# Gated network: seven products in place of eight for the output products of four steps

## The chip, the cores and the metric

The kernel runs on one core of a Trainium2 chip. The metric is the device time of one execution in microseconds (us): the median of three runs was 850.7 (849.21 to 854.43). Five engines work side by side: TensorE (PE) multiplies matrices, VectorE (DVE), ScalarE (ACT) and GpSimd (POOL) do the elementwise work, SyncE (SP) issues the transfers.

## The reference

Three stages follow each other. A retention layer over 2 batches, 8 heads, 768 positions gives x of 1536 tokens by 512. Then comes the gated network, on which the change works, then a mixture of four experts:

```python
rms = np.sqrt(np.mean(x * x, axis=-1, keepdims=True) + 1e-06)
xn = x / rms * rms_g
g = xn @ w_gate                        # 512 x 1536
silu = g * (1.0 / (1.0 + np.exp(-g)))
val = xn @ w_val                       # 512 x 1536
x2 = silu * val @ w_out                # 1536 x 512
p = probs / (probs.sum(-1, keepdims=True) + 1e-09)
out = sum(p[:, e:e+1] * (np.maximum(x2 @ w1[e], 0) @ w2[e]) for e in range(4))
```

The weights of the gated network arrive as 64-bit floating point numbers, everything is computed in float32.

## The kernel before, in words

Each float32 operand of a matmul is split into a high part `hi`, a copy rounded to the format that PE takes, and a low part `lo`, the operand less its high part. A product is then three matmuls: hi x hi, hi x lo, lo x hi.

The gated network works on 6 units (`u`) of 256 of the 1536 inner values, and on 2 groups (`g`) of 768 tokens. One pair (u, g) is a step; there are 12, and the second group is g = 1. The tokens of a group are two blocks of 384. A step has

- gate products and value products (`winograd`): seven products instead of eight, of sums of inputs and of weights. A product is 6 matmuls of 384 columns. `use` is called when a quarter of the result is ready. For the gate DVE adds two parts into one of four buffers `s` (L583) and ACT applies the activation (L587); for the value DVE adds (L613), multiplies onto the gate's quarter (L616), ACT makes the high part `hhi` (L618) and DVE or POOL the low part `hlo` (L621);
- output products (`gated_out`): for 2 blocks x 4 tiles of outputs, 2 x 3 matmuls onto one PSUM bank (L1081 to L1083), 48 in all. DVE adds each bank to the sum over units `x2acc` in SBUF (L1090).

The next step's gate products and this step's output products are placed around each other by the main loop, in a fixed order. Weights come by transfers of pieces of 256 or 512 KB through three staging buffers `wst`, in the order of `turns`. A 64-bit piece is converted by shifting bits: ACT makes `bits` (L322), DVE does three steps (L325 on `wst`, L330 on `bits`, L337 into `top`), then gate and value weights get four sums (L353), high parts on ACT (L390) and low parts on DVE or POOL (L395). Two streams of pieces alternate; each has its own `bits` buffer, and both are PSUM banks.

The kernel writes the order of instructions on every engine itself. A planner (`Pace`) keeps a clock for each engine with a cost for each task; `fill` puts waiting tasks between the matmuls of a product, `need` brings those on which the next matmul depends to their engine. Tasks marked `PV` may go to POOL or DVE. Each engine works through its list in that order and waits at an instruction until what it needs is there.

The second network (16 units, `mixed_out` and `expert_out`) follows; `mixed_out` already computes its output products for the first group as seven products, from buffers of a pool "T". From 333 us on the order is unchanged.

## Time and profile before

| | us |
|---|---|
| median of three runs (lowest, highest) | 850.7 (849.21, 854.43) |
| the profiled execution, its own time | 849.45 |
| its span in the trace | 847.7 |
| retention and normalising | about 0 to 93 |
| gated network | about 93 to 348 |
| experts | about 348 to 848 |

The span is the time between the first and the last instruction in the trace; the run's time is 1.75 us longer than it. PE's matmuls are pipelined: each of 384 columns is shown with 0.33 us, and they start 0.17 us apart.

### The profile page before, as it was taken

The numbers are of one execution on the slowest core, as the hardware profiler recorded it, in microseconds if no ns is written. First come the engines' busy times: TensorE is split into PE (matmuls) and PEld (weight loads), VectorE is DVE, ScalarE is ACT, GpSimd is POOL, SyncE is SP. The second block draws the span as 40 slices with busy tenths as digits, with TensorE's granted clock in tenths as the row PEclk, the third lists the DMA queues.
The fourth block names the chain that finished last, engine by engine and source line by source line (L and its number), as shares of the span: only waits on it lengthen the run. The fifth ranks groups of instructions, "written<-read, shape, count | busy, mean of one in ns | idle before, by whom it ended". The sixth has DMA issues, their size and how long they took to land.

```text
span 847.7 us, 13943 instructions
## 1 busy us (share of the span) xinstructions
PE 834.1 (98%) x5167; PEld 794.8 (94%) x5167; DVE 541.1 (64%) x973; ACT 432.0 (51%) x971; POOL 584.9 (69%) x713
## 2 busy tenths in 40 slices
PE   8989999999999999899999999999999999999998
PEld 7879999999999999899999999999999999999987
DVE  4886867769686847832665565466466466556664
ACT  4788765445443546665544544544545454454421
POOL 3456847364454558969789888988988988988500
PEclk9999999999999999999999999999999999999999
DMA  8951232212122100111111011010011011101003
GB/s 272 318 161 51 76 99 75 75 56 94 51 75 75 50 26 26 39 29 32 40 38 37 27 38 38 26 51 26 26 51 32 20 50 38 38 26 38 1 13 136
DMA packets 29233, 52.37 MB, mean 62 GB/s; under 512 B 3989, under 2 KB 12725, under 8 KB 29165
## 3 DMA queue, kind: packets, MB, share of 16 engines
q1 hardware_dynamic: 28880, 51.24, 19.0%
q8 instruction: 40, 0.66, 0.3%
q10 hardware_dynamic: 284, 0.24, 0.1%
q14 instruction: 29, 0.23, 0.1%
HBM read 48.33 MB, written 3.15 MB: 61 GB/s over the span
## 4 chain that ended last, share of the span: by engine, by line
PE 88%; DVE 5%; ACT 3%; POOL 1%; issue 1%; DMA 1%; SPq 0%; DVEq 0%; ACTq 0%
PE bank L523 44%; PE bank L1231 7%; PE bank L1269 6%; PE bank L1270 6%; PE bank L1268 6%; PE cross L1231 5%; PE bank L1082 3%; PE bank L1083 3%; PE bank L1081 3%; PE bank L745 2%; POOL x2Tlo L1034 1%; PE bank L727 1%; DMA qk<-in_qk_dram 1%; DVE s L616 1%; PE bank L755 1%
## 5 line engine op out<-in xcount | busy, mean ns | idle before, releaser
L532 ACT COPY kept<-bank 128x384 f32<-128x384 f32 x168 | 80.5, 479 | 121.9 <-PE bank L523 111.2
L1208 DVE SCALAR_TENSOR_TENSOR oacc<-cross,p_sb,oacc 128x256 f32<-128x256 f32 (+1 forms) x126 | 65.6, 566 | 64.2 <-PE cross L1231 64.2
L1276 DVE SCALAR_TENSOR_TENSOR oacc<-bank,p_sb,oacc 128x512 f32<-128x512 f32 (+1 forms) x97 | 72.3, 746 | 52.1 <-PE bank L1270 52.0
L1137 POOL TENSOR_TENSOR hs<-h,hs 128x384 fp32r<-128x384 f32 x97 | 97.3, 1020 | 0.8 <-ACT hs L1135 0.8
L523 PE MATMUL bank<-x2Thi,widehi 128*128 128x384 f32 x256 | 87.7, 343 | 0.7 <-DVE kept L1114 0.7
L523 PE MATMUL bank<-x2Thi,widelo 128*128 128x384 f32 x256 | 86.1, 336 | 0.0
L523 PE MATMUL bank<-x2Tlo,widehi 128*128 128x384 f32 x256 | 86.0, 336 | 0.0
L1270 PE MATMUL bank<-plainhi,hs 128*128 128x512 f32 (+1 forms) x218 | 85.1, 390 | 0.0
L1269 PE MATMUL bank<-plainlo,hs 128*128 128x512 f32 (+1 forms) x218 | 85.0, 390 | 0.0
L1268 PE MATMUL bank<-plainhi,hs 128*128 128x512 f32 (+1 forms) x218 | 84.3, 387 | 0.0
L621 POOL TENSOR_TENSOR hlo<-s,hhi 128x384 fp32r<-128x384 f32 x48 | 52.8, 1101 | 30.8 <-ACT hhi L618 24.2
L1117 ACT ACTIVATE hs<-kept 128x384 fp32r<-128x384 f32 x54 | 28.4, 526 | 87.2 <-DVE kept L1114 87.1
L1082 PE MATMUL bank<-hlo,plainhi 128*128 128x384 f32 x192 | 64.3, 335 | 1.7 <-POOL hlo L621 1.7
L523 PE MATMUL bank<-xThi,widehi 128*128 128x384 f32 x192 | 64.4, 336 | 0.0
L523 PE MATMUL bank<-xThi,widelo 128*128 128x384 f32 x192 | 64.2, 334 | 0.0
L523 PE MATMUL bank<-xTlo,widehi 128*128 128x384 f32 x192 | 64.2, 334 | 0.0
L1081 PE MATMUL bank<-hhi,plainhi 128*128 128x384 f32 x192 | 64.1, 334 | 0.0
L1083 PE MATMUL bank<-hhi,plainlo 128*128 128x384 f32 x192 | 64.1, 334 | 0.0
L1208 DVE SCALAR_TENSOR_TENSOR oacc<-bank,p_sb,oacc 128x512 f32<-128x512 f32 x84 | 59.2, 745 | 6.4 <-PE bank L1231 6.4
L464 POOL TENSOR_TENSOR downlo<-down,downhi 128x512 fp32r<-128x512 f32 x28 | 36.3, 1296 | 37.9 <-ACT downhi L460 37.9
L395 POOL TENSOR_TENSOR widelo<-sums,widehi 128x512 fp32r<-128x512 f32 x44 | 57.7, 1310 | 5.3 <-ACT widehi L390 4.9
L1143 POOL TENSOR_TENSOR h<-h 128x384 f32<-128x384 f32 x55 | 55.9, 1017 | 4.2 <-ACT h L1156 2.2
(181 smaller groups left out, 2536.5 us busy)
## 6 DMA issues: line engine op xcount, KB each, us to landing
wst<-in_moe_w_dram SPq DMA_DIRECT2D x64, 256.0 KB, 2.7
qk<-in_qk_dram SPq DMA_DIRECT2D x12, 512.0 KB, 5.7
wst<-in_moe_w_gate_dram SPq DMA_DIRECT2D x12, 512.0 KB, 3.8
wst<-in_moe_w_val_dram SPq DMA_DIRECT2D x12, 512.0 KB, 3.9
wst<-in_moe_w_out_dram SPq DMA_DIRECT2D x12, 512.0 KB, 3.7
vk<-in_vk_dram SPq DMA_DIRECT2D x10, 512.0 KB, 5.4
out_dram<-oacc SPq DMA_DIRECT2D x11, 256.0 KB, 2.0
vk<-in_vk_dram SPq DMA_DIRECT2D x2, 256.0 KB, 4.3
```

What stands on the lines that cost most here:

```text
L523: nc.tensor.matmul(out=ps, lhsT=lhs, rhs=rhs, start=(first and j == i == 0), stop=(j == KH - 1 and i == 2), skip_group_check=not first,)
L532: nc.scalar.copy(out=t, in_=ps)
L1081: nc.tensor.matmul(out=ps, lhsT=whi[:, c], rhs=hi, start=(f == 0), stop=False)
L1082: nc.tensor.matmul(out=ps, lhsT=whi[:, c], rhs=lo, start=False, stop=False)
L1083: nc.tensor.matmul(out=ps, lhsT=wlo[:, c], rhs=hi, start=False, stop=(f == NF - 1))
L1137: 0, "PV", TB, lambda eng: eng.tensor_tensor(out=lo, in0=t, in1=hi.bitcast(F32), op=ALU.subtract), [high]
L1208: run = lambda eng: eng.scalar_tensor_tensor(out=acc, in0=ps, scalar=pe, in1=acc, op0=ALU.mult, op1=ALU.add)
L1231: nc.tensor.matmul(out=where[c], lhsT=lhs[:, cols], rhs=rhs, start=bool(i == 0 and opens and opens(c)), stop=(i == 2), skip_group_check=True,)
L1268: nc.tensor.matmul(out=ps, lhsT=hi[:, c], rhs=whi[:, cols], start=(f == 0), stop=False)
L1269: nc.tensor.matmul(out=ps, lhsT=hi[:, c], rhs=wlo[:, cols], start=False, stop=False)
L1270: nc.tensor.matmul(out=ps, lhsT=lo[:, c], rhs=whi[:, cols], start=False, stop=(f == NF - 1))
L1276: nc.vector.scalar_tensor_tensor(out=acc, in0=ps, scalar=pe, in1=acc, op0=ALU.mult, op1=ALU.add)
```

## The change

For (u, 1) with u from 1 to 4 the output products are seven products of sums of the products silu x value and of sums of the output weights. Seven products times two halves of the outputs times three matmuls make 42 matmuls.

- `seven_use` takes the place of `value_use`: it makes seven operands (high and low part each) in place of four. Four more differences (`less`) of 128x384 go to POOL or DVE, and three of them overwrite a buffer `s` in place.
- `seven_out` takes the place of `gated_out`. Each product is added twice, once per half of the outputs, so DVE adds 14 banks to `x2acc` in place of 8. One bank per half ("chain") is accumulated over o1, o6, o7, o4, another ("side") over o5 and o3, then anew over o2; each partial sum is added to `x2acc` before the next product goes onto its bank.
- `out_sums` makes four sums of output weights (128x256), two high and two low parts of 512 for each of the units.
- The products are mixed one by one with the next step's gate products: v1 v2 v5 v6 v3 v7 g1 g2 v4 o1 g5 o5 g6 o3 g3 o6 g7 o7 g4 o2 o4 (v, g, o: value, gate, output).
- The `bits` of the second stream (odd pieces from the fifth on) lie in SBUF; their PSUM bank serves the chain. The buffer `sums` is double.
- In `turns` the output weights of a unit come after the gate weights of the next one.

The order holds 4821 matmuls in place of 4845; DVE has 51 instructions more, ACT 20, POOL 25, and SP issues 139 in both. The orders are alike up to about 89 us and from about 333 us on.

DVE in the second step of unit 1, from the multiplication of the quarter of v7 (L616 before, L719 after) to the first additions to `x2acc`. Before:

```order
L616 TENSOR_TENSOR s_1589<-kept_1712,s_1589 128x384 [waits DVE_49]
L353 TENSOR_TENSOR sums_1748<-sums_1748,top_1715 128x128 [waits Pool_49]
L325 TENSOR_SCALAR wst_1649<-wst_1649 128x512 [waits DMAHW7_49,Activation_49]
L583 TENSOR_TENSOR s_1784<-bank_1777,kept_1771 128x384 [waits PE_49,Activation_49]
L330 SCALAR_TENSOR_TENSOR bits_1750<-bits_1750,wst_1649 128x512 [waits DVE_49]
L616 TENSOR_TENSOR s_1618<-bank_1680,s_1618 128x384 [waits PE_49]
L325 TENSOR_SCALAR wst_1725<-wst_1725 128x512 [waits DMAHW0_49,Activation_49]
L330 SCALAR_TENSOR_TENSOR bits_1799<-bits_1799,wst_1725 128x512 [waits DVE_49]
L583 TENSOR_TENSOR s_1829<-bank_1801,kept_1818 128x384 [waits PE_49,Activation_49,Pool_49]
L583 TENSOR_TENSOR s_1841<-bank_1764,kept_1808 128x384 [waits PE_49,Pool_49]
L337 SCALAR_TENSOR_TENSOR top_1845<-wst_1649,bits_1750 128x512 [waits Pool_49]
L1090 TENSOR_TENSOR x2acc0_1222<-bank_1849,x2acc0_1222 128x384 [waits PE_49]
```

The same place now (L639 is the addition of a gate product, L699 a low part, L785 the additions to `x2acc`, two of o1 and then two of o5; L329 is a step of the weights):

```order
L719 TENSOR_TENSOR s_1859<-kept_2001,s_1859 128x384 [waits DVE_49]
L357 TENSOR_TENSOR sums_2018<-top_2004 128x128
L341 SCALAR_TENSOR_TENSOR top_2060<-wst_1887,bits_1961 128x512
L699 TENSOR_TENSOR hlo_2029<-s_1805,hhi_2028 128x384 [waits Activation_49]
L699 TENSOR_TENSOR hlo_2042<-s_1859,hhi_2041 128x384 [waits Activation_49]
L639 TENSOR_TENSOR s_2074<-bank_2063,kept_2056 128x384 [waits PE_49,Pool_49]
L719 TENSOR_TENSOR s_1898<-bank_1972,s_1898 128x384 [waits PE_49]
L785 TENSOR_TENSOR x2acc1_1221<-chain_2091,x2acc1_1221 128x384 [waits PE_49]
L785 TENSOR_TENSOR x2acc1_1221<-bank_2092,x2acc1_1221 128x384 [waits PE_49]
L329 TENSOR_SCALAR wst_1900<-wst_1900 128x512 [waits DMAHW3_49]
L785 TENSOR_TENSOR x2acc1_1221<-bank_2119,x2acc1_1221 128x384 [waits PE_49]
L785 TENSOR_TENSOR x2acc1_1221<-bank_2123,x2acc1_1221 128x384 [waits PE_49]
```

Two low parts have come in behind the multiplication, the gate's addition L639 waits for POOL, and behind it stand the value's last multiplication (L719 s_1898) and the first additions to `x2acc`; before, three weight steps (L325, L330, L337) and two gate additions stood between the value's last multiplication (L616 s_1618) and the first L1090.

DVE near 89 us, where the first gate addition of unit 0's second step stands behind weight steps (L325, L329). Before:

```order
L616 TENSOR_TENSOR s_1106<-kept_1168,s_1106 128x384 [waits DVE_49]
L325 TENSOR_SCALAR wst_716<-wst_716 128x512 [waits DMAHW2_49,Activation_49]
L325 TENSOR_SCALAR wst_993<-wst_993 128x512 [waits DMAHW7_49,Activation_49]
L583 TENSOR_TENSOR s_1244<-bank_1237,kept_1231 128x384 [waits PE_49,Activation_49,Pool_49]
L330 SCALAR_TENSOR_TENSOR bits_1195<-bits_1195,wst_716 128x512 [waits DVE_49]
L616 TENSOR_TENSOR s_1156<-bank_1123,s_1156 128x384 [waits PE_49]
L337 SCALAR_TENSOR_TENSOR top_1259<-wst_716,bits_1195 128x512 [waits DVE_49]
```

And now:

```order
L672 TENSOR_TENSOR s_1106<-kept_1168,s_1106 128x384 [waits DVE_49]
L329 TENSOR_SCALAR wst_993<-wst_993 128x512 [waits DMAHW7_49,Activation_49]
L639 TENSOR_TENSOR s_1241<-bank_1234,kept_1229 128x384 [waits PE_49,Activation_49,Pool_49]
L334 SCALAR_TENSOR_TENSOR bits_1195<-bits_1195,wst_993 128x512 [waits DVE_49]
L672 TENSOR_TENSOR s_1156<-bank_1123,s_1156 128x384 [waits PE_49]
L329 TENSOR_SCALAR wst_716<-wst_716 128x512 [waits DMAHW2_49,Activation_49]
L334 SCALAR_TENSOR_TENSOR bits_1244<-bits_1244,wst_716 128x512 [waits DMAHW4_49,DMAHW3_49,DMAHW5_49,DMAHW1_49,DMAHW6_49,DVE_49,Pool_49]
L341 SCALAR_TENSOR_TENSOR top_1279<-wst_716,bits_1244 128x512 [waits DVE_49]
```

One of the two weight steps ahead of the gate addition (L583, now L639) has moved behind the multiplication.

The diff, cut to its core (the second network's use of a shared buffer `h7` is left out):

```diff
--- before
+++ after
@@ -213,6 +213,7 @@
     HD = DM // 2
     MORE_HS = 2
     MIXED = set(range(1, N2 - 1))
+    SEVEN = {(u, g) for u in (1,2,3,4,) for g in (1,)}
     STAGED = 3
     BIG = 3
     BANKS = 6
@@ -276,7 +277,7 @@
     turns = [wides[0], wides[1], plains[0], wides[2]]
     for u in range(1, N1):
-        turns += [wides[2 * u + 1], plains[u], wides[2 * u + 2]]
+        turns += [wides[2 * u + 1], wides[2 * u + 2], plains[u]]
     turns += [wides[2 * N1 + 1], plains[N1], plains[N1 + 1]]
     for u in range(2, N2):
         turns += [wides[2 * N1 + u], plains[N1 + u]]
@@ -318,7 +319,10 @@
             w = got["t"].rearrange("p h f -> p (h f)").bitcast(U32).rearrange("p (n two) -> p n two", two=2)
             got["low"], got["high"], got["hf"] = w[:, :, 0], w[:, :, 1], w[:, :, 1].bitcast(F32)
-            got["one"] = bits_pools[second].tile([P, NC], U32, tag="bits", name="bits")
+            if second:
+                got["one"] = pools["T"].tile([P, 2 * TB], U32, tag="h7", name="bits", bufs=1)[:, 0:NC]
+            else:
+                got["one"] = psum_bits.tile([P, NC], U32, tag="bits", name="bits")
             eng.activation(out=got["one"].bitcast(F32), in_=got["hf"], func=AF.Copy, scale=REBIAS)
         def sign(eng):
@@ -344,7 +348,7 @@
-                got["s"] = wconv.tile([P, 4, P], F32, tag="sums", name="sums", bufs=1)
+                got["s"] = wconv.tile([P, 4, P], F32, tag="sums", name="sums")
@@ -414,7 +418,7 @@
-                    before = sums_done[-1:] if i == 0 else []
+                    before = (sums_done[-2:-1] if double else sums_done[-1:]) if i == 0 else []
@@ -425,6 +429,10 @@
+        if key[0] == "o" and any((key[1], x) in SEVEN for x in range(G)):
+            outs[j] = got, [hi, *lows], tops[-1][0]
+            if j == NF - 1:
+                out_sums(key[1], then)
@@ -432,6 +440,52 @@
+    outs = {}
+
+    def out_sums(u, then):
+
+        (upper, dep0, free0), (lower, dep1, free1) = outs[0], outs[1]
+        key = "S", u
+
+        def sums(eng, i):
+            (a11, a21), (a12, a22) = ((x["t"][:, 0], x["t"][:, 1]) for x in (upper, lower))
+            o, x, y, op = (
+                (a22, a21, a22, ALU.add), (a21, a11, a21, ALU.subtract),
+                (a11, a22, a11, ALU.subtract), (a12, a12, a11, ALU.subtract),
+            )[i]
+            eng.tensor_tensor(out=o, in0=x, in1=y, op=op)
+
...
+        gate = lambda: "T" in pools and (("S", u - 1) not in ready or ("S", u - 1) in used)
+        last, lows = (), []
+        for i, deps in enumerate((dep1, dep0, (), ())):
+            last = [then("PV", HD, lambda eng, i=i: sums(eng, i), *last, *deps)]
+        free0 += last
+        free1 += last
+        before = last
+        for half in range(2):
+            hi = then("A", 512, lambda eng, half=half: high(eng, half), *before, gate=gate)
+            before = [hi]
+            lows.append(then("PV", 512, lambda eng, half=half: low(eng, half), hi))
+        free0.append(lows[0])
+        free1.append(lows[1])
+        ready[key] = lows
+
@@ -463,7 +517,9 @@
-        gate = lambda: "T" in pools and (u == min(MIXED) or u - 1 in sums_used)
+        gate = lambda: "T" in pools and (
+            all(("S", x) in used for x, g in SEVEN) if u == min(MIXED) else u - 1 in sums_used
+        )
@@ -625,6 +681,117 @@
+    def seven_use(s, hs):
+        t, done, read = {}, {}, {}
+        def tile(n):
+            pool, tag = (*((pools["hp"], nm) for _ in range(5) for nm in ("hhi", "hlo")), *(
+                (pools["T"], nm) for nm in ("hx", "hx", "h00", "h01")
+            ))[n]
+            return pool.tile([P, TB], F32R, tag=tag, name=tag, bufs=5 if tag in ("hhi", "hlo") else MORE_HS if tag == "hx" else 1)
+        def operand(n, at, dep):
+            hi, lo = tile(2 * len(hs)), tile(2 * len(hs) + 1)
+            src = t[at]
+            high = pace.add(0, "A", TB, lambda eng: eng.copy(out=hi, in_=src), [dep])
+            low = pace.add(
+                0, "PV", TB, lambda eng: eng.tensor_tensor(out=lo, in0=src, in1=hi.bitcast(F32), op=ALU.subtract), [high]
+            )
+            s[at][2].extend([high, low])
+            hs[n] = hi, lo, low
+            read[at] = [high, low]
+        def less(at, x, y, *deps):
+            out, x, y = t[at], t[x], t[y]
+            done[at] = pace.add(
+                0, "PV", TB, lambda eng: eng.tensor_tensor(out=out, in0=x, in1=y, op=ALU.subtract), [*deps, *read.get(at, ())]
+            )
+        def use(f, blk, a, b):
+            at = f, blk
+            t[at], silu_task, readers = s[at]
+            silu_end = pace.need(silu_task) if silu_task else 0.0
+            if b is not None:
+                nc.vector.tensor_tensor(out=b[0], in0=a, in1=b[0], op=ALU.add)
+                pace.did("V", TB, b[1])
+                a = b[0]
+            nc.vector.tensor_tensor(out=t[at], in0=a, in1=t[at], op=ALU.mult)
+            end = pace.did("V", TB, silu_end)
+            done[at] = pace.done(end)
+            b11, b12, b21, b22 = (0, 0), (0, 1), (1, 0), (1, 1)
+            if at == b11:
+                operand(1, at, done[at])
+            elif at == b12:
+                less(b11, b12, b11, done[b12])
+                operand(5, b11, done[b11])
+            elif at == b22:
+                operand(3, b22, done[b22])
+                less(b12, b22, b12, done[b11], done[b22])
+                s[b22][2].append(done[b12])
+                operand(7, b12, done[b12])
+                less(b22, b22, b11, done[b12])
+                s[b11][2].append(done[b22])
+                operand(6, b22, done[b22])
+            else:
+                operand(2, b21, done[b21])
+                t[4], readers = pools["T"].tile([P, TB], F32, tag="h10", name="h"), []
+                s[4] = None, None, readers
+                less(4, b21, b22, done[b21], done[b22])
+                for x in (b21, b22):
+                    s[x][2].append(done[4])
+                operand(4, 4, done[4])
+            return end
+        return use
+    def values(i, hs):
+        u, g = steps[i]
+        return winograd(weights(("v", u)), xs[g], (seven_use if steps[i] in SEVEN else value_use)(silu[i], hs))
+    open_chain = []
+    def seven_out(u, g, hs):
+        w = weights(("o", u))
+        pace.need(*open_chain)
+        open_chain.clear()
+        chain = [bits_pools[1].tile([P, 512], F32, tag="bits", name="chain"), bank()]
+        at = [[], banks.readers[-1]], [[], []]
+        side = [None, None]
+        order = ((1, 0, 0), (5, 1, 1), (3, 0, 1), (6, 0, 1), (7, 1, 1), (2, 0, 0), (4, 1, 0))
+        for n, half, blk in order:
+            onto = n in (5, 3, 2)
+            pace.matmuls(0, pace.need(hs[n][2]))
+            if n == 5:
+                tw = weights(("S", u))
+            for j in range(KH):
+                if n == 5:
+                    side[j], at[1][j] = bank(), banks.readers[-1]
+                ps = (side if onto else chain)[j][:, 0:TB]
+                pace.matmuls(0, pace.need(*at[onto][j]))
+                if n in (1, 2, 4):
+                    which = w[0 if n == 1 else 1]
+                    c = (HD if n == 4 else 0) + j * P
+                    whi, wlo = (x[:, c:c + P] for x in which)
+                else:
+                    whi, wlo = (x[:, {6: 0, 7: 1, 3: 2, 5: 3}[n], j * P:(j + 1) * P] for x in tw)
+                hi, lo, _ = hs[n]
+                for k, (lhs, rhs) in enumerate(((whi, hi), (whi, lo), (wlo, hi))):
+                    nc.tensor.matmul(
+                        out=ps, lhsT=lhs, rhs=rhs, start=(k == 0 and n in (1, 5, 2)), stop=(k == 2), skip_group_check=True,
+                    )
+                pace.matmuls(3 * MM)
+                acc = x2acc[g][:, blk * KD + half * KH + j, :]
+                at[onto][j].append(pace.add(
+                    1, "V", TB, lambda eng, acc=acc, ps=ps: eng.tensor_tensor(out=acc, in0=ps, in1=acc, op=ALU.add),
+                    [pace.done(pace.now)], port=False,
+                ))
+                open_chain.append(at[onto][j][-1])
+            if n == 3 and g == max(x for y, x in SEVEN if y == u):
+                w_used(("S", u))
+            if n == 4 and g == G - 1:
+                w_used(("o", u))
+            pace.fill(3 * KH * MM)
+            yield
@@ -1305,9 +1476,14 @@
         hs = {} if i else first_hs
         pace.tight = u == N1 - 1
         if i:
-            some(gate, 1)
+            if steps[i - 1] in SEVEN:
+                for _ in range(5):
+                    next(before)
+                    next(gate)
+            else:
+                some(gate, 1)
             if i == 1:
-                value = winograd(weights(("v", u)), xs[g], value_use(silu[i], hs))
+                value = values(i, hs)
                 some(value, 1)
             some(before, 2)
             whole(gate)
@@ -1315,19 +1491,19 @@
                 w_used(("g", u))
             whole(before)
             if i > 1:
-                value = winograd(weights(("v", u)), xs[g], value_use(silu[i], hs))
+                value = values(i, hs)
                 some(value, 1)
             some(value, 1)
         if i + 1 < len(steps):
-            gate = gate_products(i + 1)
-            next(gate)
+            gate = gate_products(i + 1, steps[i] in SEVEN)
+            some(gate, 2 if steps[i] in SEVEN else 1)
         else:
             hidden = hidden_products(0, 0, first)
             next(hidden)
         whole(value)
         if g == G - 1:
             w_used(("v", u))
-        before = gated_out(u, g, hs)
+        before = (seven_out if steps[i] in SEVEN else gated_out)(u, g, hs)
         if i == 5:
             nc.vector.tensor_reduce(out=p_sum, in_=p_raw, axis=mybir.AxisListType.X, op=ALU.add)
             nc.vector.tensor_scalar(out=p_sum, in0=p_sum, scalar1=PEPS, scalar2=None, op0=ALU.add)
```

## Rows read from the trace of the kernel before

**Rows 1.** Page, part 1: busy us, share of the span, instructions.

```profile
PE 834.1 (98%) x5167; PEld 794.8 (94%) x5167; DVE 541.1 (64%) x973; ACT 432.0 (51%) x971; POOL 584.9 (69%) x713
```

**Rows 2.** Windows: stretch, length, PE, PEld, DVE, ACT, POOL busy, clock, DMA, GB/s.

```profile
120.00:320.00 200.00, 199.78 (x1146) 198.33 (x1145) 142.28 (x266) 97.04 (x214) 100.19 (x125) 1.00 0.20 64
```

**Rows 3.** Timeline of PE: start us, us, engine, line, output<-inputs; one output step.

```profile
307.87 0.33 PE L1081 MATMUL bank<-hhi,plainhi 128*128 128x384 f32 x1
...
311.86 0.33 PE L1083 MATMUL bank<-hhi,plainlo 128*128 128x384 f32 x1
```

**Rows 4.** Groups by line and form, DVE: busy us, mean ns, idle before.

```profile
L1090 DVE TENSOR_TENSOR x2acc<-bank,x2acc 128x384 f32<-128x384 f32 x64 | 35.4, 552 | 22.4 <-PE bank L1083 22.4
...
L616 DVE TENSOR_TENSOR s<-kept,s 128x384 f32<-128x384 f32 x36 | 26.5, 735 | 1.2
...
L337 DVE SCALAR_TENSOR_TENSOR top<-wst,bits 128x512 uint32<-128x512 uint32 x36 | 24.1, 678 | 0.3
...
L325 DVE TENSOR_SCALAR wst<-wst 128x512 uint32<-128x512 uint32 x36 | 21.1, 589 | 7.6 <-ACT bits L322 7.0
L613 DVE TENSOR_TENSOR kept<-bank,kept 128x384 f32<-128x384 f32 x36 | 19.9, 553 | 21.1 <-PE bank L523 17.2 <-ACT xThi L815 2.4 <-ACT bits L322 1.1
L583 DVE TENSOR_TENSOR s<-bank,kept 128x384 f32<-128x384 f32 x36 | 19.7, 553 | 16.1 <-PE bank L523 8.2 <-POOL hlo L621 3.9 <-ACT bits L322 3.6
...
L616 DVE TENSOR_TENSOR s<-bank,s 128x384 f32<-128x384 f32 x12 | 6.6, 548 | 1.3 <-PE bank L523 1.3
```

**Rows 5.** The same view, POOL.

```profile
L1143 POOL TENSOR_TENSOR h<-h 128x384 f32<-128x384 f32 x55 | 55.9, 1017 | 4.2 <-ACT h L1156 2.2
...
L395 POOL TENSOR_TENSOR plainlo<-wst,plainhi 128x512 fp32r<-128x512 f32 x32 | 41.9, 1330 | 1.2 <-ACT plainhi L390 1.2
```

**Rows 6.** The same view, ACT.

```profile
L618 ACT CAST hhi<-s 128x384 fp32r<-128x384 f32 x48 | 24.7, 514 | 18.4 <-DVE s L616 18.0
```

**Rows 7.** Tile s: ns minimum/median/maximum, first and last start.

```profile
L621 POOL TENSOR_TENSOR hlo<-s,hhi x48: 992/1022/1331, 83.7 to 348.0; 128x384 fp32r<-128x384 f32 x48
...
L616 DVE TENSOR_TENSOR s<-kept,s x36: 557/559/1586, 82.0 to 342.6; 128x384 f32<-128x384 f32 x36
```

**Rows 8.** Timeline near 158 us, POOL and DVE.

```profile
158.09 1.31 POOL L621 TENSOR_TENSOR hlo<-s,hhi 128x384 fp32r<-128x384 f32 x1 [1.45 <-ACT hhi L618]
...
158.44 1.25 DVE L325 TENSOR_SCALAR wst<-wst 128x512 uint32<-128x512 uint32 x1
...
159.35 1.48 POOL L395 TENSOR_TENSOR widelo<-sums,widehi 128x512 fp32r<-128x512 f32 x1
...
160.07 0.68 DVE L330 SCALAR_TENSOR_TENSOR bits<-bits,wst 128x512 uint32<-128x512 uint32 x1
```

**Rows 9.** Timeline near 90 us, DVE, ACT and PE.

```profile
89.15 2.39 DVE L325 TENSOR_SCALAR wst<-wst 128x512 uint32<-128x512 uint32 x2
91.46 0.55 DVE L583 TENSOR_TENSOR s<-bank,kept 128x384 f32<-128x384 f32 x1
91.93 0.69 DVE L330 SCALAR_TENSOR_TENSOR bits<-bits,wst 128x512 uint32<-128x512 uint32 x1
...
92.04 0.52 ACT L587 ACTIVATE s<-s 128x384 f32<-128x384 f32 x1 [2.27 <-DVE s L583]
92.47 0.46 ACT L532 COPY kept<-bank 128x384 f32<-128x384 f32 x1
...
92.98 0.44 PE L523 MATMUL bank<-xB22hi,widehi 128*128 128x384 f32 x1 [1.38 <-ACT kept L532]
```

**Rows 10.** Timeline near 346 us, POOL and PE.

```profile
345.15 1.96 POOL L621 TENSOR_TENSOR hlo<-s,hhi 128x384 fp32r<-128x384 f32 x2
...
346.20 0.44 PE L1082 MATMUL bank<-hlo,plainhi 128*128 128x384 f32 x1 [1.57 <-POOL hlo L621]
```

**Rows 11.** Timeline near 323 us, POOL and PE.

```profile
321.20 1.99 POOL L621 TENSOR_TENSOR hlo<-s,hhi 128x384 fp32r<-128x384 f32 x2
323.16 0.45 POOL L353 TENSOR_TENSOR sums<-sums,wst 128x128 f32<-128x128 f32 x1
...
325.55 0.33 PE L1081 MATMUL bank<-hhi,plainhi 128*128 128x384 f32 x1
...
326.42 0.33 PE L1083 MATMUL bank<-hhi,plainlo 128*128 128x384 f32 x1
```

25 lines of the change are left out of this document (21 added, 4 removed).

## The prediction

> **What bounds the kernel now.** I read the shares of busy time first: TensorE (PE) is busy for 98% of the span, the other engines for 51 to 69% [rows 1]. A share is an average, so the stretches come next: of the 200 us from 120 to 320 PE is busy for 199.78, at a granted clock of 1.00, while DVE is busy for 142.28 and POOL for 100.19 [rows 2]. The whole change lies between 89 and 333 us, so nearly all of it falls where PE does nothing but matmuls, one behind the other. Matmuls saved there are worth their full time, and any new wait of PE costs its full time too. Two old waits of PE stand at the edges of the changed part: 1.38 us at 92.98 [rows 9] and 1.57 us at 346.20 [rows 10].
>
> Times come from one profiled execution (849.45 us; span 847.7). The median of the runs shown, 850.7, lies 1.25 above it. The sum is made against 849.45 and 1.25 is added at its end.
>
> **Matmuls taken away.** In four steps (second group of units 1 to 4) 48 matmuls become 42: 24 fewer. The price of one is the distance from start to start: 307.87 to 311.86 are 23 such steps [rows 3], 3.99 / 23 = 0.1735 us. 24 x 0.1735 = 4.16 us, all on the path. **-4.16.** Sums of output weights (units 1 to 4) add no matmul.
>
> **What DVE, ACT and POOL get for it.** By the order of instructions DVE gets 51 more, ACT 20, POOL 25. Spread over the changed part that fits: DVE has 200 - 142.28 = 57.7 us free in 200, and 51 x 0.55 (the size of the commonest addition) = 28 [rows 2, 4]; POOL has 99.8 free and gets about 25 x 1.02 = 25.5 [rows 5]; ACT 103 free, 20 x 0.514 = 10.3 [rows 6]. So over the whole they cost nothing. But the load is not spread: it stands in four stretches, each from the first value product to the last output product, 21 products of 6 matmuls, 21 x 1.04 = 21.9 us. There DVE has 41 instructions, by their mean rows about 24 us less some 0.08 of overlap at each start (91.46 + 0.55 is past the next start, 91.93 [rows 9]): DVE is nearly full exactly there. That cover is gone, and I walk it.
>
> **The walk** (t = 0 at the first matmul of the value products; order v1 v2 v5 v6 v3 v7 g1 g2 v4 o1 g5 o5 g6 o3 ...). A product is 6 x 0.1735 = 1.04 us.
> - v3 is the fifth product and ends at 5 x 1.04 + 0.16 (a matmul's 0.33 less 0.17 [rows 3]) = 5.36. DVE adds 0.553 and multiplies 0.735 [rows 4]: 6.65. POOL's first difference, 1.02 [rows 5]: 7.67.
> - DVE does v7 behind it, 0.553 + 0.735: 7.95. POOL's second difference: 8.97.
> - ACT copies the high parts of two operands, 0.514 each [rows 6]: about 8.7. DVE has one sum and one weight step of 0.678 [rows 4] in front, then two low parts at 0.56 to 0.735 (the same shape, both inputs in SBUF, as the multiply): about 10.1 to 10.4.
> - Only then may POOL's third difference overwrite the block: 11.1 to 11.4. It must, because DVE's next instruction, the addition of gate product g2, goes into a buffer of the same ring and waits for POOL.
> - This is the wait that the change adds, and behind it in DVE's queue stand the addition itself (0.553), the last value multiply (0.548), both additions of o1 (0.552 each), a weight step (0.589) and the first addition of o5 (0.552): together 3.35 [rows 4]. So the addition of o5 ends at 14.5 to 14.8, or some 0.4 earlier with the overlaps.
> - PE wants to begin o3 at 13 x 1.04 = 13.5, and o3 accumulates on top of o5's sum in the same bank, so it waits for that addition.
>
> PE is late by 1.1 us at the means. With the commonest multiply of 0.559 in place of the mean 0.735 [rows 7] and the overlaps it is 0.2. With long forms it is more: multiply 1.586 [rows 7] (+0.85), three POOL differences at 1.331 [rows 7] (+0.93), a weight step at 1.25 [rows 8] (+0.66): 3.5. I take 1.1, since the mean rows hold slow instances as often as that trace had them. Further on in the stretch the margins are 0.1 to 0.5 us and I find no second stall. **+4 x 1.1 = +4.4**, bounds 4 x 0.2 = 0.8 and 4 x 3.5 = 14.0.
>
> Why some instances are long can be seen: at 158.44 a weight step took 1.25 beside POOL's 1.31 of 158.09, while at 160.07 the step whose input `bits` is in PSUM took 0.68 beside POOL's 1.48 of 159.35 [rows 8]. The change moves the `bits` of one of the two streams of converted weights from PSUM to SBUF, and gives POOL 16 differences inside the very stretches walked. The Trainium skill, "SBUF — State Buffer", section "Who interferes with whom", has a rule for this that speaks against the change: a DVE instruction with two SBUF inputs, or in a mode that uses both its ports, shares an exclusive lock with a POOL instruction that reads SBUF, and the later one stands still until the other has ended. The two rows at 158 us agree with it; by it the sum would be that of the third rival below.
>
> **The start.** PE's 1.38 at 92.98 goes back to DVE: two weight steps of 1.2 each (2.39 from 89.15) stand ahead of the gate addition at 91.46, then ACT's activation (92.04) and copy (92.47) [rows 9]. With the next gate weights loaded earlier, one weight step stands there in place of two. One step is worth 1.2, the stall 1.38: I take **-1.0**, bounds 0 and -1.38.
>
> **The end.** PE's 1.57 at 346.20 is POOL being behind, its 1.96 us pair starting at 345.15 [rows 10]. The first weights of the second network are then converted earlier, POOL has less before it: **-0.7**, half of it, bounds 0 and -1.57.
>
> **Output weights later.** They now come one piece of work later. For the last unit POOL's low part of the second quarter moves behind the pair of 321.20, which ends at 323.19; with 0.46 for a sum and 1.33 [rows 5] it is ready at 325.0, and the first matmul with it starts at 326.42 [rows 11]. Hidden by 1.4 us; uncovered it would cost what exceeds that. The DMA queue issues as many transfers as before (139), in another order, and I find no weight that comes late. Nothing.
>
> **The sum:** 849.45 - 4.16 + 4.4 - 1.0 - 0.7 = 848.0; + 1.25 = **849.2 us**. Lower end: 849.45 - 4.16 + 0.8 - 1.38 - 1.57 = 843.1 (+ 1.25 = 844.4). Upper: 849.45 - 4.16 + 14.0 = 859.3 (860.5); with the two gains at what I took for them, 858.8.
>
> **Rivals.**
> 1. *DVE's queue has slack* (late by under 0.5 per stretch). For it: the median of the multiply is 559 ns, its mean is pulled up by few [rows 7]; against it: 41 instructions in 21.9 us, and the wait for POOL ahead of six of them. With 0.2: 849.45 - 4.16 + 0.8 - 1.7 = 844.4, 845.6 at the median. Chance 0.28.
> 2. *DVE becomes the bound, slower.* Both multiplies long (+1.7), three long differences (+0.93), a long weight step (+0.66): 1.1 + 3.3 = 4.4 per stretch: 849.45 - 4.16 + 17.6 - 1.7 = 861.2, at the median 862.4. It decides from 3.6 per stretch, where the time is 1% above the old one (859.2). For it: all these lengths occur [rows 7, 8] and more POOL work meets them; against it: they would have to meet every time. Chance 0.10.
> 3. *Each meeting of DVE and POOL blocks the later one.* In the walk about two DVE instructions per stretch start inside a POOL one, and lose on average half of its 1.02: 1.1 + 1.0 = 2.1: 849.45 - 4.16 + 8.4 - 1.7 = 852.0, 853.2 at the median. For it the row at 158.44, against it that the means hold a part of it already. Chance 0.17.
> 4. *The change does not do what it says*: the order has 24 matmuls fewer, so hardly; 0.01.
>
> **How the numbers follow.** My forecast (0.5 to 1.6 late per stretch, 846.8 to 851.2) has 0.44. What can be told from no change is about 1%, 8.5 us: under 842.2 lies only what no term gives (0.04, out of rival 1, for gains that I do not see); over 859.2 the second rival, less its lower part (0.08). The rest, 0.88, is within 1%. The range 844.0 to 858.5 holds the forecast, rivals 1 and 3 and the long forms; it leaves out most of rival 2 and a gain beyond the bounds, about 0.14.
>
> **What would show it.** Right: four idle times of PE before o3's first product of about 1 us, released by DVE's addition of o5, and the gate addition before it released by POOL; 4821 matmuls in the order; the stall at 92.98 near 0.4, that at 346.20 near 0.9. If PE shows no idle time in the four stretches, rival 1; if DVE multiplies of over 1 us stand in each, rival 2 or 3. Wrong in another way: waits of PE outside the stretches, for weights (sums of output weights, output weights) or for banks.

## The result, and the profile after

The change makes the kernel slower: 859.73 us (six runs, 858.7 to 861.25) against 850.25, ratio 1.0106, 95% interval 1.0088 to 1.0125. The forecast was 849.2, range 844.0 to 858.5. The profiled execution took 860.63 us, its span is 858.8. Executions far longer than their fellows (1170.68 to 4185.04 us: one of the kernel before, one each of one_stream, share_new_place and shift1) are left out of all times below, and as it was the profiled one in one_stream and shift1, no trace of these two is read.

The page's busy shares and two windows of the changed kernel (columns as in [rows 1, 2]):

```profile
PE 836.9 (97%) x5143; PEld 793.5 (92%) x5143; DVE 574.3 (67%) x1024; ACT 440.7 (51%) x991; POOL 626.7 (73%) x738
...
120.00:320.00 200.00, 189.43 (x1063) 184.81 (x1063) 166.76 (x310) 100.28 (x219) 130.77 (x140) 0.99 0.19 59
136.00:140.00 4.00, 3.44 (x11) 3.45 (x12) 2.62 (x6) 1.60 (x4) 3.77 (x4) 0.57 0.05 19
```

Where PE had been busy for 199.78 of 200 us it is now busy for 189.43, though the clock fell as well: from 136 to 140 us it was granted 0.57, near the lower of its two levels (1.2 of 2.4 GHz). The list of PE's waits, with what each waited for (total us, times, longest), says where the time is:

```profile
PE bank L579 <- ACT kept L588: 5.0, 7, 1.4
PE bank L779 <- DVE x2acc L785: 3.6, 4, 1.4
PE bank L779 <- DVE s L639: 3.2, 4, 1.0
...
PE bank L1249 <- POOL hlo L677: 0.9, 2, 0.7
...
PE chain L779 <- DVE x2acc L785: 0.3, 1, 0.3
...
PE bank L579 <- DVE kept L669: 0.2, 1, 0.2
```

L779 are the new output products, L579 gate and value products. To add it up, restarts after a wait included, I took the distance of every two neighbouring matmuls less 0.1735 us, from 85 to 375 us:

| lost on PE, us | before | after |
|---|---|---|
| new output products (the four stretches) | - | 9.5 |
| gate and value products | 4.0 | 8.4 |
| old output products | 2.3 | 1.5 |
| matmuls at the lower clock | 0 | 1.5 |
| sum, expert rows included | 6.5 | 20.9 |

20.9 - 6.5 - 4.16 (24 matmuls) = 10.2 of the 11.1 us by which the span grew. So there are two losses: about 9.5 us inside the four stretches, and more than 5 outside them. The spans compare a profiled execution below its median with one above it: the medians are 9.5 us apart.

**Inside a stretch.** Timeline of the first, DVE, POOL and PE (the order shown ahead of the prediction, here with its times):

```profile
163.18 0.87 DVE L719 TENSOR_TENSOR s<-kept,s 128x384 f32<-128x384 f32 x1
...
164.18 0.68 DVE L341 SCALAR_TENSOR_TENSOR top<-wst,bits 128x512 uint32<-128x512 uint32 x1
164.20 1.53 POOL L708 TENSOR_TENSOR s<-s 128x384 f32<-128x384 f32 x1 [0.56 <-DVE s L719]
164.78 2.10 DVE L699 TENSOR_TENSOR hlo<-s,hhi 128x384 fp32r<-128x384 f32 x2
165.69 0.77 POOL L357 TENSOR_TENSOR sums<-top,sums 128x128 f32<-128x128 f32 x1
167.02 1.01 POOL L708 TENSOR_TENSOR s<-s 128x384 f32<-128x384 f32 x1 [0.56 <-DVE hlo L699]
...
168.07 0.56 DVE L639 TENSOR_TENSOR s<-bank,kept 128x384 f32<-128x384 f32 x1 [1.19 <-POOL s L708]
...
168.68 0.45 PE L779 MATMUL bank<-hhi,sumshi 128*128 128x384 f32 x1 [0.70 <-DVE s L639]
169.01 0.55 DVE L785 TENSOR_TENSOR x2acc<-chain,x2acc 128x384 f32<-128x384 f32 x1
...
170.46 1.01 DVE L785 TENSOR_TENSOR x2acc<-bank,x2acc 128x384 f32<-128x384 f32 x2
...
171.15 0.41 PE L779 MATMUL bank<-hhi,sumshi 128*128 128x384 f32 x1 [0.61 <-DVE x2acc L785]
```

The two low parts, 1.1 to 1.5 us in my walk, took 2.10 between POOL's second difference (1.53 in place of 1.02) and a weight sum. POOL's third difference ends at 168.03, DVE's gate addition waits 1.19 us for it, and PE waits twice: at 168.68 before the second half of o5, whose bank that gate addition still reads, and at 171.15 before o3. Both waits are in all four stretches. The two low parts take 2.10 in the second stretch too, 1.28 and about 1.8 in the others.

**Outside.** ACT, DVE, POOL and PE near 134 us, in a step without the new products:

```profile
131.13 1.47 POOL L399 TENSOR_TENSOR plainlo<-top,plainhi 128x512 fp32r<-128x512 f32 x1
131.38 1.77 DVE L341 SCALAR_TENSOR_TENSOR top<-wst,bits 128x512 uint32<-128x512 uint32 x1
...
133.18 0.62 ACT L394 CAST plainhi<-top 128x512 fp32r<-128x512 f32 x1 [1.75 <-DVE top L341]
...
133.71 0.47 ACT L588 COPY kept<-bank 128x384 f32<-128x384 f32 x1
...
134.24 0.44 PE L579 MATMUL bank<-xB22hi,widehi 128*128 128x384 f32 x1 [1.43 <-ACT kept L588]
...
136.56 0.69 PE L579 MATMUL bank<-xThi,widehi 128*128 128x384 f32 x1 [1.01 <-ACT kept L588]
137.04 0.52 PE L579 MATMUL bank<-xTlo,widehi 128*128 128x384 f32 x1
```

DVE's last weight step, now with both inputs in SBUF, takes 1.77 us beside POOL. ACT waits for it with a weight's high part, and the copy `kept` for which PE waits stands behind that in ACT's queue. After two such waits the matmuls are 0.32 us apart in place of 0.1735 for some ten of them. Only this execution was traced; three of the six show a granted clock of 0.998 (860.3 to 861.25 us) and three 1.0 (858.7 to 859.17), which fits a fall that only some of them had. The wait near 110 us has another head: a weight's high part on ACT waits 1.72 us for POOL's sums, and the copy stands behind it.

DVE's groups after, for [rows 4]:

```profile
L341 DVE SCALAR_TENSOR_TENSOR top<-wst,bits 128x512 uint32<-128x512 uint32 x36 | 30.3, 842 | 2.5 <-POOL sums L357 2.2
L334 DVE SCALAR_TENSOR_TENSOR bits<-bits,wst 128x512 uint32<-128x512 uint32 x36 | 27.5, 764 | 0.4
L329 DVE TENSOR_SCALAR wst<-wst 128x512 uint32<-128x512 uint32 x36 | 26.5, 742 | 7.6 <-ACT bits L326 7.2
...
L719 DVE TENSOR_TENSOR s<-kept,s 128x384 f32<-128x384 f32 x12 | 9.4, 784 | 0.4
...
L699 DVE TENSOR_TENSOR hlo<-s,hhi 128x384 fp32r<-128x384 f32 x8 | 7.3, 953 | 0.0
```

The last weight step rose from 678 to 842 ns on average, the first from 589 to 742. The low parts, a form that DVE did not have before, take 953 on average: beyond the 559 to 735 that I bounded them with.

### The profile page after: what moved, and what is told of

The parts are those of the page before. It is cut to its first block, busy times and chain, and to the rows that moved or that the text cites. A ratio compares the mean times of both kernels' runs of the same rounds, so it can differ in the third digit from the quotient of the medians.

```text
span 858.8 us, 13976 instructions
## 1 busy us (share of the span) xinstructions
PE 836.9 (97%) x5143; PEld 793.5 (92%) x5143; DVE 574.3 (67%) x1024; ACT 440.7 (51%) x991; POOL 626.7 (73%) x738
## 4 chain that ended last, share of the span: by engine, by line
PE 78%; DVE 11%; POOL 4%; ACT 4%; issue 3%; DMA 1%; DVEq 0%; POOLq 0%; ACTq 0%
PE bank L579 38%; PE bank L1402 7%; PE bank L1440 6%; PE bank L1441 6%; PE bank L1439 6%; PE cross L1402 5%; PE bank L779 2%; PE bank L912 2%; PE bank L1249 1%; PE bank L1250 1%; PE bank L1248 1%; POOL widelo L399 1%; DVE s L672 1%; POOL sums L357 1%; PE bank L894 1%
## 5 line engine op out<-in xcount | busy, mean ns | idle before, releaser
L579 PE MATMUL bank<-x2Thi,widehi 128*128 128x384 f32 x256 | 87.7, 342 | 0.7 <-DVE kept L1281 0.7
L579 PE MATMUL bank<-x2Thi,widelo 128*128 128x384 f32 x256 | 86.1, 336 | 0.0
L579 PE MATMUL bank<-x2Tlo,widehi 128*128 128x384 f32 x256 | 85.9, 336 | 0.0
L399 POOL TENSOR_TENSOR widelo<-sums,widehi 128x512 fp32r<-128x512 f32 x47 | 61.7, 1312 | 13.0 <-PE bank L579 11.0
L579 PE MATMUL bank<-xThi,widehi 128*128 128x384 f32 x192 | 65.1, 339 | 1.2 <-ACT kept L588 1.0
L579 PE MATMUL bank<-xThi,widelo 128*128 128x384 f32 x192 | 64.6, 337 | 0.0
L579 PE MATMUL bank<-xTlo,widehi 128*128 128x384 f32 x192 | 64.6, 336 | 0.0
L1302 ACT CAST hs<-h 128x384 fp32r<-128x384 f32 x98 | 48.8, 513 | 16.6 <-POOL h L1310 15.3
L1325 DVE TENSOR_TENSOR h<-bank,kept 128x384 f32<-128x384 f32 x42 | 23.3, 555 | 45.1 <-PE bank L579 44.5
L579 PEld LDWEIGHTS bank<-x2Thi,widehi 128*128 128x128 f32 x256 | 48.2, 188 | 4.4 <-DVE kept L1281 3.0
L399 POOL TENSOR_TENSOR widelo<-wst,widehi 128x256 fp32r<-128x256 f32 x64 | 37.3, 608 | 18.1 <-ACT widehi L394 18.1
```

Of the source, the lines that this page charges most:

```text
L399: eng.tensor_tensor(out=at(lo), in0=t, in1=at(hi).bitcast(F32), op=ALU.subtract)
L579: nc.tensor.matmul(out=ps, lhsT=lhs, rhs=rhs, start=(first and j == i == 0), stop=(j == KH - 1 and i == 2), skip_group_check=not first,)
L1302: high = pace.add(0, "A", TB, lambda eng: eng.copy(out=hi, in_=t), [dep])
```

## The experiments

Each time is the median, each ratio that to the kernel before, with its 95% interval. What is lost on PE is added up as in the table above.

**Which part loses outside the stretches.** All 48 matmuls everywhere, the rest of the change kept:

```diff
-    SEVEN = {(u, g) for u in (1,2,3,4,) for g in (1,)}
+    SEVEN = set()
```

> The change without its seven products: all steps keep their 48 output matmuls, while the bits of the second stream in SBUF, the double buffer of sums and the new order of loads stay. Theory 1 (all that is lost is lost in the four stretches, through DVE's queue): no wait of PE outside the edges, 849 to 851 us, as before the change. Theory 2 (bits in SBUF make DVE and POOL block each other, so that weight steps and the copies behind them come late) and theory 3 (the new order of loads makes conversions late): PE's waits for ACT's copies at about 110, 134 and 137 us, 3.5 us in the change, are still there, 853 to 858 us.

852.03 us, 1.0012 [0.9994, 1.0029]. PE's waits of 1.10, 1.37 and 0.99 us near 110, 134 and 137 us are there as in the change. So these do not belong to the seven products. PE's waits for ACT's copies in no_seven:

```profile
PE bank L579 <- ACT kept L588: 3.7, 4, 1.4
```

They are 4 in place of 7. The later ones of the change (191.62, 288.03 and 335.53, and one for DVE at 284.23; 2.6 us with restarts) come only with the seven products. And no_seven is no slower than the kernel before beyond its interval: shorter waits at the two edges pay for a part of the new ones. The whole change is about 8 us slower than no_seven (1.0106 against 1.0012), so most of the time is lost with the seven products: 9.5 + 2.6 - 4.16 = 7.9. Next, the `bits` of the second stream back in PSUM, with the test by which that stream starts:

```diff
-            if second:
-                got["one"] = pools["T"].tile([P, 2 * TB], U32, tag="h7", name="bits", bufs=1)[:, 0:NC]
-            else:
-                got["one"] = psum_bits.tile([P, NC], U32, tag="bits", name="bits")
+            got["one"] = bits_pools[second].tile([P, NC], U32, tag="bits", name="bits")
...
-            last = then("A", NC, bits, last, *ones[second][-1:], gate=lambda: not second or "T" in pools)
+            last = then("A", NC, bits, last, *ones[second][-1:], gate=lambda: second in bits_pools)
```

> As no_seven, but both streams' bits lie in PSUM as before the change; what is left of the change is the order of loads and the double buffer of sums. Theory 2: back to 849 to 851 us, DVE's last weight step (L341) never over 1 us. Theory 3: as slow as no_seven, 853 to 858 us.

847.51 us, 0.9958 [0.9943, 0.9974]: the three waits are gone, and it is faster than the kernel before, though the old wait at the start is back (1.37 us at 94.04). The order of loads was tried by itself, the bits in SBUF:

```diff
-        turns += [wides[2 * u + 1], wides[2 * u + 2], plains[u]]
+        turns += [wides[2 * u + 1], plains[u], wides[2 * u + 2]]
```

> As no_seven, but with the old order of loads; the bits stay in SBUF. Theory 2: as slow as no_seven, 853 to 858 us, with weight steps of over 1.2 us. Theory 3: back to 849 to 851 us.

851.51 us, 1.0015 [0.9995, 1.0036], as slow as no_seven, but not by the same waits: of the three only the first is left (1.09 us at 108.70), those near 134 and 137 us are gone, and the old wait at the end is back (1.56 us at 347.31), with a fall of the clock behind it. So the new order has a part in two of the three waits, and gains as much elsewhere. Then the buffer of sums, single as before:

```diff
-                got["s"] = wconv.tile([P, 4, P], F32, tag="sums", name="sums")
+                got["s"] = wconv.tile([P, 4, P], F32, tag="sums", name="sums", bufs=1)
...
-                    before = (sums_done[-2:-1] if double else sums_done[-1:]) if i == 0 else []
+                    before = sums_done[-1:] if i == 0 else []
```

> no_seven (48 output matmuls everywhere, bits of the second stream in SBUF, new order of loads) with one buffer of sums as before. If bits in SBUF alone make the waits at 110, 134 and 137 us: they stay, 851 to 853. If these need the second buffer of sums as well, which lets POOL's weight work run ahead into DVE's: gone, 847 to 850.

848.12 us, 0.9975 [0.9966, 0.9985]: the three waits are gone. Mean time of DVE's last weight step in no_seven, in no_seven_psum_bits and in no_seven_sums1:

```profile
L341 DVE SCALAR_TENSOR_TENSOR top<-wst,bits 128x512 uint32<-128x512 uint32 x36 | 26.6, 739 | 2.4 <-POOL sums L357 2.2
```

```profile
L338 DVE SCALAR_TENSOR_TENSOR top<-wst,bits 128x512 uint32<-128x512 uint32 x36 | 24.4, 679 | 2.0 <-POOL widelo L396 1.8
```

```profile
L341 DVE SCALAR_TENSOR_TENSOR top<-wst,bits 128x512 uint32<-128x512 uint32 x36 | 28.1, 780 | 0.2
```

In PSUM the step takes 679 ns, in SBUF 739 and 780. The shortest, the median and the longest (ns), in no_seven and in no_seven_sums1:

```profile
L341 DVE SCALAR_TENSOR_TENSOR top<-wst,bits x36: 671/680/1778, 24.6 to 315.7; 128x512 uint32<-128x512 uint32 x36
```

```profile
L341 DVE SCALAR_TENSOR_TENSOR top<-wst,bits x36: 670/680/1501, 24.4 to 311.4; 128x512 uint32<-128x512 uint32 x36
```

So the step itself is as fast from SBUF; a few instances are long. With one buffer of sums the mean is the longest of the three, yet PE does not wait. So both edits are needed for the three waits, and the new order of loads too for the last two. That a long step costs only where ACT's copies stand behind it is how I read the order, with the step of 1.77 us above as the example; no run moves such a step alone. The same edit to the whole change:

> The change with one buffer of sums as before (the other edit of ring5_sums1), four buffers s. If the gain of ring5_sums1 (3.5 us) is that of the fifth buffer s: 859 to 862 us. If it came from the order that the single buffer makes: 855 to 857.

855.56 us, 1.0053 [1.0038, 1.0068], 4 us less than the change. Its new output products still lose 9.9 us: the loss inside is separate. From no_seven_sums1 to sums1, the seven products alone, the time rises by 6.6 (by the ratios) to 7.4 us (by the medians).

**What is late inside.** First the ring: a fifth buffer `s`, in sums1 (the room comes from the sums), takes away the gate addition's wait for POOL's third difference:

```diff
-    kept_places, silu_places = Places(pace, 3), Places(pace, 4)
+    kept_places, silu_places = Places(pace, 3), Places(pace, 5)
...
-            t = tp.tile([P, TB], F32, tag="s", name="s", bufs=4)
+            t = tp.tile([P, TB], F32, tag="s", name="s", bufs=5)
```

> The whole change with five buffers s in place of four, so that the first gate addition in a stretch no longer waits for POOL's third difference; the buffer of sums is single again to make room. If that wait is what fills DVE's queue (my prediction's step): PE's waits on the gate addition (3.2 us in the change) go, those before o3 (3.6 us) fall to 0 to 1.5, time 852 to 856 us. If DVE's work alone fills the stretch (41 instructions in 21.9 us), the waits only move to later products of it, time 857 to 860 us.

856.27 us, 1.0061 [1.0038, 1.0084]. Against sums1 it gains nothing. The wait at the gate addition is gone, and another has come in its place, in three of the four stretches before o6 and for POOL's low part (in the second stretch 2.08 us before o3; timeline of PE in the first):

```profile
168.59 0.44 PE L779 MATMUL chain<-hlo,sumshi 128*128 128x384 f32 x1 [1.14 <-POOL hlo L699]
```

**Bits in PSUM with the seven products.** The second stream and the chain take turns on one bank (share; new tests in the planner's gates, some ten lines), and in a second kernel the third difference has a buffer of its own, all differences on POOL:

```diff
-                less(b22, b22, b11, done[b12])
+                t[6] = pools["T"].tile([P, 2, TB], F32, tag="h7", name="h", bufs=1)[:, 0]
+                less(6, b22, b11, done[b12])
```

> The whole change, with two streams and both streams' bits in PSUM: the second stream and the chain take turns on one bank, and the planner keeps the second stream's pieces out while a chain is open. DVE's order in the stretches is nearly that of the change, instruction by instruction. If meetings over the bits in SBUF are only the loss outside the stretches: 855 to 856 us (4.5 less), waits of PE in the stretches 8 to 9.5 us as in the change. If they also lengthen the queue inside: waits there 4 to 7 us, 851 to 854 us.

> share, with the third difference written to a buffer of its own (free now) and no longer over the block that two low and high parts still read; all differences on POOL. POOL's third difference then ends about 2 us earlier, and the gate addition behind it on DVE too. If that wait is the head of the queue: PE's waits on the gate addition (0.7 to 1.0 a stretch) vanish, those before o3 fall under 0.5, in sum 3 to 6 us less than share: 846 to 850 us. If DVE's work decides: no more than 2 us less than share.

863.90 (1.0143 [1.0119, 1.0167]) and 864.16 us (1.0145 [1.0118, 1.0171]). In the second and third stretch PE now waits 6.6 and 5.4 us for a weight step that must end before the chain may have the bank. The other two can be read: the fourth loses 1.8 us at o5 and o3, as it does in the change, the first 1.2 in place of 1.6. So bits in SBUF are at most a part of what makes a stretch late. share_new_place has no wait at o5, but 1.2 and 1.6 us at o3 in place of 1.2 and 1.8 at both.

**One stream.** Every piece uses the first stream's bits in PSUM:

```diff
-        second = n % 2 if n >= 4 else 0
+        second = 0
```

> The whole change with all weights in one stream: every piece takes its bits from the PSUM buffer of the first stream, none from SBUF; the chain keeps its bank. Theory 2 (the bits in SBUF cost the waits outside the stretches: 4.5 us between no_seven and no_seven_psum_bits): about 855 us, with PE's waits in the four stretches as they are (9 us). If the bits in SBUF also lengthen DVE's queue inside the stretches: 851 to 854, the waits there below 7 us. If one stream makes conversions late: over 858, with PE waiting for weights.

> ring5_sums1 (five buffers s, one of sums) with one stream of bits in PSUM. If the two causes are separate their savings add up: 856.3 less about 3 to 4.5, 852 to 853 us. If the ring's wait was only the place where contention showed, it gains less, 854 to 856.

860.24 (1.0121 [1.0106, 1.0135]) and 867.42 us (1.0199 [1.017, 1.0227]). In the second, PE waits 3.6 us for ACT's and 2.9 for POOL's parts of output weights: one stream converts too late. Of the first only the time is known.

**Weight work kept out.** A flag closes the planner's gate for weight tasks on DVE and POOL from the first value product to o3:

```diff
-            last = then("V", NC, sign, last, port=False)
+            last = then("V", NC, sign, last, gate=lambda: not quiet[0], port=False)
...
+                quiet[0] = steps[i] in SEVEN
```

> The whole change, bits in SBUF as in it, but the planner may issue no weight step, sum or low part of weights on DVE and POOL from the first value product of a stretch to o3. If the queue of DVE (its work and meetings with POOL there) makes o5 and o3 late: PE's waits in the four stretches fall from 9 us to under 4, 852 to 856 us, some of it given back where weights come later. If only the wait for POOL's third difference counts, those waits stay at 6 to 9 us, 857 to 861.

> All three together: one stream of bits in PSUM, five buffers s with one of sums, no weight work on DVE and POOL in the first part of the stretches. If these are the whole loss, what is left is the saving of 24 matmuls: 844 to 848 us, faster than the kernel before. If conversions that wait become late elsewhere, 849 to 854.

880.79 (1.0353 [1.034, 1.0367]) and 893.62 us (1.0516 [1.0502, 1.053]). The new output products lose 5.7 and 2.2 us in place of 9.5, and output weights come late by far more: 22.2 us of waits in the second, up to 4.4 each.

**Moving the products.** In sums1 each gate product goes ahead of its output product (shift1); in shift2 by two, with o2 ahead of o7:

```diff
-                    next(before)
                     next(gate)
+                    next(before)
```

> sums1 with the mix moved by one product: each gate product comes ahead of its output product (v4 g5 o1 g6 o5 g3 o3 ...), so that o5 and o3 come one product (1.04 us) later against the same queue on DVE; no other instruction is added or left out. If the head of the stretch (gate addition behind POOL, last value multiply, additions) is late by a fixed 2 us: PE's waits there fall from 2.1 to 2.9 us a stretch to 1 to 1.9, 851 to 853 us against 855.6. If DVE's and POOL's whole work in the stretch is more than it can take, the wait comes back at the later output products: 854 to 857.

> As shift1, moved by two products: v4 g5 g6 o1 g3 o5 g7 o3 g4 o6 o2 o7 o4. Fixed lateness at the head: those waits fall to 0 to 0.9 a stretch, 847 to 850 us, below the kernel before. Too much work in all: 854 to 858, with waits of the last products (chain) in place of those of o5 and o3.

868.54 (1.0231 [1.0203, 1.0258]) and 863.93 us (1.0167 [1.0154, 1.018]). Why shift1 is the slower of the two stays open. In shift2 PE waits longer before o3 than with less room, 1.9, 3.4, 1.9 and 0.9 us. DVE's timeline in its first stretch:

```profile
162.99 0.68 DVE L334 SCALAR_TENSOR_TENSOR bits<-bits,wst 128x512 uint32<-128x512 uint32 x1
...
163.59 1.25 DVE L329 TENSOR_SCALAR wst<-wst 128x512 uint32<-128x512 uint32 x1
...
164.76 0.55 DVE L785 TENSOR_TENSOR x2acc<-chain,x2acc 128x384 f32<-128x384 f32 x1
...
165.69 0.54 DVE L639 TENSOR_TENSOR s<-bank,kept 128x384 f32<-128x384 f32 x1
166.16 0.68 DVE L334 SCALAR_TENSOR_TENSOR bits<-bits,wst 128x512 uint32<-128x512 uint32 x1
...
166.75 1.01 DVE L785 TENSOR_TENSOR x2acc<-bank,x2acc 128x384 f32<-128x384 f32 x2
```

The planner fills the room: three weight steps and a gate addition stand ahead of o5's additions (166.75). Neither of my two theories had that.

**Only DVE's three weight steps held**, from the multiplication after v3 to o3 (same gate as quiet, on three tasks, in sums1); the same with five buffers `s`; and the same with the old order of loads:

> sums1 (855.6 us), and the planner keeps DVE's three weight steps (and nothing else) out of each stretch from the multiplication after v3 to the end of o3; in unit 1 that takes a step of about 0.6 and one of 0.7 us, and their meetings with POOL, from the queue ahead of o5's additions. If these steps are what makes the head late: PE's waits at o5 and o3 fall from 2.1 to 2.9 us a stretch to 1.0 to 1.6, 851 to 853 us. If the waits of DVE and POOL on each other are all of it: no more than 0.5 a stretch less, 854 to 856. Held steps that come late elsewhere: over 856, with PE waiting for output weights.

> The same with five buffers s, so that the gate addition has no wait for POOL and only it and the value multiply stand ahead of o1's additions on DVE. Each alone left another wait behind (the fifth buffer gave nothing: POOL's low parts were late in its place). If the two together free the head: waits of the stretches under 1.2 us each, 847 to 851 us, near or below the kernel before. If POOL's own work, 9 pieces of 1.0 us before o6, is the bound: PE waits for POOL's low parts, 1.2 to 2 a stretch, 852 to 856.

> hold_steps with the old order of loads, so that a unit's output weights come ahead of the next gate weights. In hold_steps PE's waits in the stretches were down to about 3.6 us in all (9.9 in sums1), and 10 us came back as waits for ACT's copies and for output weights. If those came back because output weights stand last in the loads: they shrink to under 4, 848 to 853 us. If the held steps (three per piece, 0.6 to 0.7 us each) are simply missing time on DVE and POOL: they come back at other weights, 856 to 868 us.

865.31 (1.0175 [1.0138, 1.0211]), 861.61 (1.0133 [1.0098, 1.0168]) and 860.60 us (1.0133 [1.0112, 1.0153]). PE's waits in hold_steps:

```profile
PE bank L580 <- ACT kept L589: 5.1, 5, 1.5
PE bank L1252 <- ACT plainhi L394: 4.5, 4, 2.3
PE bank L1254 <- POOL plainlo L399: 2.0, 5, 0.5
...
PE bank L781 <- DVE s L640: 1.2, 2, 0.7
...
PE bank L781 <- DVE x2acc L787: 0.9, 1, 0.9
```

The new output products (L781) lose 5.0 us with their restarts in place of 9.9, and output weights come late by more than that. With five buffers `s` too, the new output products have one wait left in each stretch, before o6 and for POOL's low part (PE's waits in hold_steps_ring5):

```profile
PE chain L781 <- POOL hlo L700: 5.2, 4, 1.7
```

So with the weight steps and the ring's wait both out of the way POOL is the late one, as the second theory had it. With the old order of loads the waits for output weights go, as expected, but the time does not fall to the 848 to 853 that went with that: the stretches lose 8.9 again, with none of the three weight steps in DVE's queue there. So holding the steps does not by itself free a stretch, and the 5.0 above is not the weight steps' share. In the second stretch the low parts and POOL's third difference are late as before:

```profile
207.88 2.14 DVE L700 TENSOR_TENSOR hlo<-s,hhi 128x384 fp32r<-128x384 f32 x2
208.83 0.78 POOL L357 TENSOR_TENSOR sums<-top,sums 128x128 f32<-128x128 f32 x1
210.17 1.00 POOL L709 TENSOR_TENSOR s<-s 128x384 f32<-128x384 f32 x1 [0.56 <-DVE hlo L700]
...
211.20 0.56 DVE L640 TENSOR_TENSOR s<-bank,kept 128x384 f32<-128x384 f32 x1 [1.17 <-POOL s L709]
```

**The planner's marks.** The steps that read bits were marked as free of POOL, as they are with bits in PSUM:

```diff
-            last = then("V", NC, body, last, port=False)
+            last = then("V", NC, body, last, port=bool(second))
```

> The whole change, and the planner is told that the second and third weight steps of the second stream meet POOL (they read two inputs in SBUF now; the change left them marked as free of it, which they were in PSUM). If the waits outside the stretches (7 us with the clock's fall) come from the planner not knowing: they shrink, 853 to 857 us. If knowing does not help, since the meetings cost the same wherever they stand: 858 to 862.

877.77 us, 1.0321 [1.0288, 1.0355]. The stretches lose 4.8 us, the old output products about 20, waiting for output weights: a planner that knows of the meetings moves the steps, and the weights are late.

## Why the prediction was wrong

- **24 matmuls, 4.16 us:** right. The distance is unchanged.
- **Start, -1.0:** the number was right (0.20 at 92.52, a gain of 1.2 us), and one weight step stands there in place of two, but the reason was not the order of loads. With the new order and bits in PSUM (no_seven_psum_bits) both steps and the wait are there; with the old order and bits in SBUF (no_seven_old_turns) the wait is as short as in the change:

```profile
90.20 2.40 DVE L326 TENSOR_SCALAR wst<-wst 128x512 uint32<-128x512 uint32 x2
...
94.04 0.44 PE L576 MATMUL bank<-xB22hi,widehi 128*128 128x384 f32 x1 [1.37 <-ACT kept L585]
```

```profile
91.56 0.45 PE L579 MATMUL bank<-xB22hi,widehi 128*128 128x384 f32 x1 [0.22 <-ACT kept L588]
```

It is the move of the bits that took a step away. The number was luck.
- **End, -0.7:** right, 0.9 us gained, and by the order of loads: the wait is 0.66 in no_seven and 1.56 in no_seven_old_turns.
- **"+4 x 1.1 = +4.4", PE late in each stretch:** the largest step that failed. The mechanism was right (third difference, gate addition, DVE's queue, o3), the size was not: 9.5 us, 2.4 a stretch, within its bounds of 0.8 to 14. By o3 PE is 1.7 to 2.5 us late and not 1.1. In the first two stretches the low parts cost 2.1 and not 1.1 to 1.5; and the walk left out that o5's second half needs the bank which that gate addition frees, so that PE is late there already, by 0.7 to 1.0 us. The third rival's 2.1 a stretch is the nearest. The trace agrees with the rule of the Trainium skill ("SBUF — State Buffer", "Who interferes with whom") that a DVE instruction with two SBUF inputs contends with a POOL instruction that reads SBUF: the two low parts take 2.10 us beside POOL's 1.53 and 0.77.
- **Nothing for PE's waits outside the stretches:** the other step that failed. Late output weights were put at nothing, and in the change no wait of PE is for them; but the sum has no term for the bits in SBUF and the second buffer of sums outside the stretches, nor for late gate and value products behind a stretch. The first cost 3 to 4.6 us (no_seven against no_seven_sums1 and no_seven_psum_bits), the lower clock in some executions included; the second 2.6 us, by the trace. I took the bits' change of place into account as a cause of long forms inside the stretches alone, and there it does little.
- **The two together:** by the runs the seven products cost about 8 us, where the sum had 0.2 (4.4 less 4.16), and the rest of the change about 1, within its interval of none, where the sum had -1.7. Either alone would have stayed below 858.5.
- **Slower by over 1% had 0.08**, for a rival that laid it all on the stretches. The time came out of both.

So the gain of 4.16 us is paid for on DVE and POOL: the seven products need 51 and 25 more instructions mostly in the same short stretches in which the next unit's weights must be converted. That these two compete is shown by quiet, hold_steps and port_known: the stretches lose less, and output weights come late by more. Not shown is whether any order can hold both; none tried did. Of all kernels no_seven_psum_bits is the fastest, 847.51 us: none of the seven products, with the new order of loads and the second buffer of sums.

## What to carry to other kernels

Matmuls saved at full PE are worth their full time, but price the elementwise work that buys them in the stretch where it falls, beside what else must be done there, and not against idle time averaged over the phase. When a wait is taken away, look for the next instruction in the same queue before counting it as won: a fifth buffer, a new place and a later due time each only moved it. A buffer moved from PSUM to SBUF is an edit of its own, to be measured by itself. And two kernels that take the same time need not wait at the same places: no_seven and no_seven_old_turns do not.
